# A hand-ordered attention and MLP kernel: state fetch and state transpose moved up in the head, and a new order of work for the first three batches

## The chip, the core and the metric

The kernel runs on one core of a Trainium2 chip. The core has four compute engines with queues of their own: TensorE (PE in the profile, with its weight loads shown apart as PEld), VectorE (DVE), ScalarE (ACT) and GpSimd (POOL). SyncE (SP) only issues DMA transfers; ACT and POOL issue some too. Each engine works through its own list of instructions in the order in which the kernel's source issues them, and waits at an instruction until the data and buffers that it needs are there.

The metric is the time of one execution on the device in microseconds. Before the change it is 201.53 us, the median of three runs between 201.45 and 201.57.

## The reference

Cut to what matters:

```python
B, H, S, Ns, D = 8, 8, 512, 32, 64            # batches, heads, tokens, state rows, head width
scores  = (x @ state^T) / sqrt(D)             # per batch and head: 512 x 32
a       = softmax(scores, -1);  xread = a @ state
scores2 = (state @ x^T) / sqrt(D)             # the same products, 32 x 512
a2      = softmax(scores2, -1); sread = a2 @ x
rows    = concat([xread, sread], tokens)      # 544 rows of 512 (heads x D) per batch
h       = rows @ w_in                         # 512 -> 2048
out     = maximum(0.01 * h, h) @ w_out        # 2048 -> 512
```

The inputs are x (8 MB, float32), the state, w_in and w_out (4 MB each, float32); the output has 4352 rows of 512 float32 numbers.

## The kernel before

The kernel never forms xread. For each batch it builds M = state times w_in (a 256 x 2048 matrix, in four column chunks c = 0 to 3; `a_m`, L381 to L398, an "M product" of eight small matmuls, whose PSUM tile is called `pm`), and the first layer is then `aT` (the transposed probabilities) times M: `ff1` (L409 to L421) makes one of 16 blocks j of 128 hidden units for 512 tokens in PSUM tile `ph`, and a leaky ReLU on ACT ("relu") moves it to `hT`. The second layer multiplies `hT` with `w_out`. For batch 0 it does this with plain matmuls, `piece(b, hT, i, jq)` (L693) for token tile i and hidden blocks 4*jq to 4*jq+3; `part` picks some of the four, and `y_store` moves a finished tile out. From batch 1 on it uses a scheme of seven products instead of eight (`Fast` and `Batch`), cut into 56 "units" of two matmuls each; `before.run(1)` or `u` issues one unit of the previous batch. That scheme needs sums of `w_out` blocks (`weights_sum(dst, m0, m1)`, L730, tiles `tw`, each half made on DVE or POOL) and sums of `hT` blocks (`before.f.sums`, DVE, tiles `su`).

Scores come from `a_scores(a)` (L219), which needs the transposed x (`xT`) and the transposed state. Batch 0 has its own path: `x0_t` transposes x on TensorE, scores and softmax are done in two halves of 256 tokens (`scores0` to `probs0`), and the first layer in quads of four blocks (`Quad`, L1036). For batch 1, `turn` (L1091) transposes x on TensorE. From batch 2 on, x is loaded (`load_x`, into `xl`), cast to bfloat16 head by head (`cast_x`, into `xb`; for batch 2 half on ACT, half on POOL) and transposed by DMA (`a_xt_dma`, L208). Softmax over state rows runs on DVE and ACT: `a_top`, `a_rows`, `a_less` (maximum and subtraction), `a_exp` (ACT), `a_probs` (sum, reciprocal, product: `aT`). Softmax over tokens: `a_max2` (DVE, `mcol`), `a_exp2` (ACT, one call per half), `a_probs2`; its result `e2` is transposed by DMA with `a_a2t`.

The states of batches 0 and 1 come in one transfer at the start. The states of batches 2 and 3 are group 0, those of 4 to 7 group 1: `load_state(i)` (L177) fetches a group in eight small transfers from SP into `stf`, and `state_t(i)` (L186) scales and casts it on POOL (`stb`) and issues a DMA transpose from SP into `st_t`. The memset of two columns of `stf[0]` on DVE (L1088) comes before the fetch of group 0, which overwrites them and therefore waits for it: the place of the memset in DVE's order is what starts the fetch.

Nothing plans this at run time. Order is written by hand: the head (batches 0 and 1, and the first half of batch 2) as a list of calls, and the stretches for b = 2 and later as strings of tokens, `FIRST` for b = 2 and `ORDER` after it. In these strings `u` is a unit, `f.j` an ff block, `r.j` its relu, `mk.c` an M product, `ev.c.g.A` or `.V` its cast by ACT or DVE, `S` the scores of the next batch, `tp`, `rw`, `ls`, `ex`, `x2`, `rc`, `ml` the parts of its softmax, `rows` the product of `e2` with x for finished batches (PSUM tile `psn`), `casts.h` two heads' casts on POOL, `st` is `state_t(1)`, `a2t` and `turn` are DMA transposes, `sb` and `sn` block sums, `d.n` the saving of product n (`d.1.A` by ACT), and `l4` the load of x for batch 4.

PSUM has eight banks: two for tag `ph`, two for `py`, and two each for the single tiles `big` and `sc`. A tile can be written again only when its last reader is done, which ties TensorE to ACT and DVE.

DMA transfers that POOL issues (`w_in`, `w_out`, x of batches 1 and 2) are all queued by 22 us, in this order at their end: `w_out` chunk 2, two halves of x of batch 2, two halves of `w_out` chunk 3.

Of the kernel before, what the change touches and what calls it, by code (L numbers as in the profile page):

```python
# [9 lines left out]
P = 128  # L10
# [20 lines left out]
def kernel(  # L31
# [100 lines left out]
    def load_w_out(c, parts=1):  # L132
        n = 4 // parts
        for j in range(4 * c, 4 * (c + 1), n):
            nc.gpsimd.dma_start(
                w_out_bf[:, j:j + n, :],
                moe_w_out[P * j:P * (j + n), :].rearrange("(j p) f -> p j f", p=P),
            )
# [147 lines left out]
    def a_top(a):  # L286
        a.m1 = block_max(a.sc[:].rearrange("p g c -> p (g c)"), NB)
# [582 lines left out]
    pxt = {}  # L870

    def x0_t(u, k):
        b = k // 3
        if (u, b) not in pxt:
            pxt[u, b] = psum.tile([P, 3 - 2 * b, 2, P], BF16, name="pxth", tag=("ph", "py")[u])
# [36 lines left out]
    def spread0(dst, parts, start):  # L912
        for i, part in enumerate(parts):
            for q in range(2):
                for v in range(2):
                    for c in range(NK):
                        n = H * v + NK * q + c
                        nc.tensor.matmul(
                            dst[NS * c:NS * (c + 1), q, P * v:P * (v + 1)],
                            lhsT=part[:, n:n + 1].to_broadcast([P, NS]),  # L920
                            rhs=ident[:], start=start, stop=start or (q == v == i == 1),
                        )
# [8 lines left out]

    def split0(m, eng):
        hi = att.tile([P, NG], BF16, name="hi0", tag="hi0")
        VEC(hi[:], m[:])
        lo = att.tile([P, NG], BF16, name="lo0", tag="lo0")
        with nc.allow_low_precision(reason="the second of two parts of one fp32 value"):
            eng.tensor_tensor(out=lo[:], in0=m[:], in1=hi[:], op=ALU.subtract)
        return hi, lo
# [19 lines left out]
    def recip0(u):  # L958
        q = att.tile([P, NG], BF16, name="q0", tag="q0")
        with nc.allow_low_precision(reason="one rounding, of the finished reciprocal"):  # L960
            nc.vector.reciprocal(q[:], r0[u][:])
        return q

    def recip0_rows(u, q):
        qb0[u] = psum.tile([P, 2, HT], FP32, name="qb0", tag="ph")
        spread0(qb0[u], (q,), True)
# [6 lines left out]
    for c in range(3):  # L973
        load_w_in(c)
    cast_x0(0, 0, NT, VEC)
    for k in (1, 2):
        cast_x0(k, 0, 2, VEC)
    for k in (1, 2):
        cast_x0(k, 2, NT, VEC)
    cast_x0(3, 0, 2, VEC)  # L980
    cast_x0(3, 2, NT, POO)
    for u, k in ((0, 0), (1, 0), (0, 1), (0, 2), (1, 1), (1, 2), (0, 3), (1, 3)):
        x0_t(u, k)
    for u in range(2):
        xt0_evict(u, 0, SCA)
        xt0_evict(u, 1, VEC)
# [3 lines left out]
    for v in range(2):  # L990
        scores0(0, v)
        max0(0, v)
    m = split0(m0[0], nc.gpsimd)
    load_w_in(3)
    load_w_out(0)
    for u in range(2):
        nc.gpsimd.dma_start(
            a1.xb[:, NK * u:NK * (u + 1)].rearrange("p h t d -> p h (t d)"),
            x[1, NK * u:NK * (u + 1)].rearrange("h (p t) d -> p h (t d)", t=NT),
        )  # L1000
    load_w_out(1, 2)
    load_w_out(2)
    for h in (0, NK):
        load_x(2, nc.gpsimd, h, h + NK)
    load_w_out(3, 2)
    rows0(0)
    scores0(1, 0)
    max0(1, 0)
    rows0(1)
    spread0(scn[0], m, False)  # L1010
    exp0(0)
    scores0(1, 1)
    max0(1, 1)
    for u in range(2):
        eps0(u)
    pm = a_m(a0, 0, "big")
    SCA(a0.M[:, 0, :DM], pm[:, 0, :])
    sum0(0)
    m = split0(m0[1], nc.vector)
    q = recip0(0)  # L1020
    spread0(scn[1], m, False)
    exp0(1)
    recip0_rows(0, q)
    VEC(a0.M[:, 1, :DM], pm[:, 1, :])
    probs0(0)
    pm1 = a_m(a1, 0, "sc")
    sum0(1)
    q = recip0(1)
    pm = a_m(a0, 1, "big")
    for g in range(2):  # L1030
        SCA(a0.M[:, g, DM:2 * DM], pm[:, g, :])
# [33 lines left out]
    def m0_evict(c, pm):  # L1065
        for d in range(DM * c, DM * (c + 1), 2 * P):
            VEC(a0.M[:, :, d:d + 2 * P], pm[:, :, d - DM * c:d - DM * c + 2 * P])

    first = Quad(0, 0, "py")
    first.product(range(2))  # L1070
    recip0_rows(1, q)
    probs0(1)
    m_evict(a1, 0, pm1, VEC)
    first.product(range(2, 4))
    first.relu()
    for u, j, tag in (
        (0, 4, "ph"), (1, 0, "big"), (1, 4, "py"), (0, 8, "ph"), (1, 8, "py"), (0, 12, "ph"), (1, 12, "big"),
    ):
        quad = Quad(u, j, tag)
        quad.product()  # L1080
        quad.relu()
# [32 lines left out]
    piece(0, h0, 1, 0)  # L1114
    piece(0, h0, 0, 0)
    a_exp2(a0, 0)
    turn(0)
    open_xb(2)
    weights_open()
    wide = psum.tile([P, 2, DM], FP32, name="pyw", tag="big", bufs=1)  # L1120
    VEC(a1.xT[:, :, 0:2, :], pt[0][:])
    turn(1)
    a_exp2(a0, 1)
    piece(0, h0, 2, 0, bank=wide[:, 0])
# [5 lines left out]
    m_take(a1, 1, 0, SCA)  # L1130
# [5 lines left out]
    piece(0, h0, 3, 1, copy=None, part=(0, 1))  # L1136
    piece(0, h0, 1, 1, copy=None, part=(0, 1))
    weights_sum(2, 0, 4, nc.gpsimd)
    a_open(a2, 2)
    m_take(a1, 1, 1, VEC)  # L1140
    m_take(a1, 2, 0, SCA)
    piece(0, h0, 3, 1, copy=None, part=(2, 3))
    piece(0, h0, 3, 2, copy=None, part=(0, 1))
    piece(0, h0, 2, 2, copy=None, part=(0, 1))
# [7 lines left out]
    cast_x(2, 4, 5, POO)  # L1152
    cast_x(2, 5, 6, POO)
    cast_x(2, 6, 7, POO)
    a_max2(a1)
    a_probs(a1, 0)
    a_probs(a1, 1)
    cast_x(2, 7, 8, POO)
    weights_sum(2, 4, 8)
    a_xt_dma(a2, slice(1, 2))  # L1160
    weights_sum(1, 4, 8)
    weights_sum(3, 4, 8, nc.gpsimd)
    a_exp2(a1, 0)
    weights_sum(1, 0, 4, nc.gpsimd)
    weights_sum(0, 4, 8, nc.gpsimd)
# [3 lines left out]
    piece(0, h0, 2, 2, copy=None, part=(2, 3))  # L1169
    piece(0, h0, 0, 1, copy=None, part=(2, 3))  # L1170
    cast_x(3, 0, 2, POO)
    a_exp2(a1, 1)
    piece(0, h0, 3, 2, copy=None, part=(2, 3))
# [404 lines left out]
```

## Time and profile before

| | before |
|---|---|
| median of three runs | 201.53 us (201.45 to 201.57) |
| the profiled execution's own time | 201.61 us |
| its span, first to last instruction | 199.8 us |
| TensorE busy | 193.8 us (97%) |
| DVE, ACT, POOL busy | 164.8, 150.1, 63.9 us |
| mean granted TensorE clock | 0.998 |
| moved by DMA | 27.50 MB |

In rows of the timeline the columns are: start in us from the span's start, duration in us, engine, line of the kernel (L181 is line 181), operation, output tile <- input tiles, shape, number of instructions merged into the row, and in brackets how long the engine had been idle before it and what ended that. A merged row's duration is the busy time of its instructions. The tile view gives the time "to landing" of a DMA transfer, counted from the start of its issue instruction; a transfer has landed when its consumers may read it. In the table by stretches, each engine's busy time in that stretch is followed by its number of instructions, and the DMA share is that of the core's 16 DMA engines.

### The profile page before, as it was taken

To read this page: it belongs to the slowest core of one execution; us is meant where nothing else is said; L and a number is where in the kernel's file an instruction comes from. 1 tells how busy PE (TensorE), PEld (TensorE's weight loads), DVE (VectorE), ACT (ScalarE), POOL (GpSimd) and SP (SyncE) were. 2 spreads that over 40 slices of the span, in tenths; PEclk is the share of its full clock that TensorE was granted. 3 is DMA by queue.
4 is the path that set the end of the run, shared out by engine and by line. 5 is a ranking of instruction groups with operands and counts; after the bars stand their busy time and mean duration, and the time that the engine had idled before them with its cause. 6 is when DMAs were issued, how large, how long until landed. Compare 5 with 4: busy or idle time off the path is not lost.

```text
span 199.8 us, 5151 instructions
## 1 busy us (share of the span) xinstructions
PE 193.8 (97%) x2106; PEld 136.5 (68%) x2106; DVE 164.8 (82%) x282; ACT 150.1 (75%) x286; POOL 63.9 (32%) x90
## 2 busy tenths in 40 slices
PE   7999998999999999999999999999999999999993
PEld 2566533446677667767777777777777788799882
DVE  2676498599999998997999899999899877995613
ACT  3478628599779649997899779996999768767710
POOL 8473284790009102720413040500050024005350
PEclk9999999999999999999999999999999999999999
DMA  6999997999571998398293614080013401310026
GB/s 203 212 207 192 199 292 136 206 318 162 101 220 27 197 276 165 58 255 268 51 259 113 184 22 85 3 262 0 3 51 159 82 3 76 134 56 0 5 82 182
DMA packets 40616, 27.50 MB, mean 138 GB/s; under 512 B 25424, under 2 KB 37840, under 8 KB 40592
## 3 DMA queue, kind: packets, MB, share of 16 engines
q1 hardware_dynamic: 34032, 20.35, 39.7%
q0 software_dynamic: 5728, 6.03, 16.8%
q10 hardware_dynamic: 832, 0.79, 1.2%
q8 instruction: 16, 0.26, 0.6%
q14 instruction: 8, 0.07, 0.1%
HBM read 17.30 MB, written 8.91 MB: 131 GB/s over the span
## 4 chain that ended last, share of the span: by engine, by line
PE 90%; DMA 4%; DVE 3%; POOL 0%; issue 0%; ACT 0%; ACTq 0%
PE yq L770 43%; PE ph L414 18%; PE pm L393 4%; PE pf L492 3%; PE yu L770 3%; PE pl L660 3%; PE ph L1051 3%; DMA st_t<-stb 2%; DMA xf<-in_x_dram 2%; PE py L699 2%; PE pl L581 2%; PE pyw L699 1%; PE psn L359 1%; PE sc L225 1%; PE php L1051 1%; PE phw L427 1%
## 5 line engine op out<-in xcount | busy, mean ns | idle before, releaser
L420 ACT ACTIVATE hT<-ph 128x512 bf16<-128x512 f32 x84 | 49.1, 608 | 14.3 <-PE ph L414 14.3
L770 PEld LDWEIGHTS <-su 128*128 128x128 bf16 x480 | 46.2, 98 | 12.4 <-ACT hT L420 0.4
L414 PE MATMUL ph<-aT,M 128*128 128x512 bf16 x168 | 47.9, 379 | 0.0
L770 PEld LDWEIGHTS <-hT 128*128 128x128 bf16 x336 | 32.3, 98 | 12.0 <-issue 2.7
L770 PE MATMUL yq<-tw_xf,su 128*128 128x256 bf16 x224 | 30.8, 273 | 0.0
L770 PE MATMUL yq<-w_out_bf,hT 128*128 128x256 bf16 x224 | 29.2, 273 | 0.0
L114 POOL CAST xb<-xl 128x512 bf16<-128x512 f32 (+1 forms) x24 | 15.2, 673 | 20.9 <-DMA xl<-in_x_dram 20.9
L414 PEld LDWEIGHTS <-M 128*128 128x128 bf16 x168 | 16.0, 98 | 7.7 <-issue 1.9
L759 DVE TENSOR_TENSOR su<-hT 128x1024 bf16<-128x1024 bf16 x28 | 19.1, 686 | 2.6 <-ACT hT L420 2.5
L842 POOL TENSOR_TENSOR yo<-sv,sv 128x512 f32<-128x512 f32 x7 | 9.3, 1330 | 37.2 <-ACT e L313 31.4
L1283 ACT CAST M<-pm 128x512 bf16<-128x512 f32 x30 | 16.8, 596 | 0.6 <-PE pm L393 0.6
L779 ACT COPY sv<-yq 128x512 f32<-128x512 f32 x24 | 14.0, 587 | 3.4 <-PE yq L770 3.3
L770 PE MATMUL yq<-tw_x,su 128*128 128x256 bf16 x112 | 16.3, 273 | 0.0
L770 PE MATMUL yq<-w_out_bf,su 128*128 128x256 bf16 x112 | 15.3, 273 | 0.0
L782 DVE TENSOR_TENSOR yo<-yq,sv 128x512 f32<-128x512 f32 x20 | 13.5, 677 | 2.1 <-PE yq L770 2.1
L770 PE MATMUL yq<-tw_x,hT 128*128 128x256 bf16 x104 | 13.9, 273 | 0.0
L313 ACT ACTIVATE e<-sc,mcol 128x512 bf16<-128x512 f32 x16 | 11.2, 704 | 0.2 <-DVE mcol L307 0.2
L699 PEld LDWEIGHTS <-hT 128*128 128x128 bf16 x64 | 5.9, 98 | 7.4 <-issue 0.9
L759 DVE TENSOR_TENSOR su<-su,hT 128x1024 bf16<-128x1024 bf16 x14 | 10.6, 755 | 0.2
L672 ACT COPY ls<-pl 128x512 f32<-128x512 f32 x16 | 9.5, 592 | 1.5 <-PE pl L660 1.0
L307 DVE TENSOR_REDUCE mcol<-sc 128x2 f32<-128x1024 f32 x8 | 9.7, 1216 | 0.0
L235 DVE TRANSPOSE_TENSOR_REDUCE mrow<-sc 128x32 f32<-128x1024 f32 x7 | 8.7, 1243 | 0.5 <-PE sc L225 0.5
(193 smaller groups left out, 350.8 us busy)
## 6 DMA issues: line engine op xcount, KB each, us to landing
xl<-in_x_dram SPq DMA_DIRECT2D x5, 1024.0 KB, 6.6
out_dram<-yo SPq DMA_DIRECT2D x10, 512.0 KB, 2.9
w_in_bf<-in_moe_w_in_dram POOLq DMA_DIRECT2D x4, 512.0 KB, 7.9
out_dram<-yo SPq DMA_DIRECT2D x7, 256.0 KB, 2.7
w_out_bf<-in_moe_w_out_dram POOLq DMA_DIRECT2D x2, 512.0 KB, 12.8
w_out_bf<-in_moe_w_out_dram POOLq DMA_DIRECT2D x4, 256.0 KB, 13.1
xl<-in_x_dram POOLq DMA_DIRECT2D x2, 512.0 KB, 15.4
out_dram<-ysb SPq DMA_DIRECT2D x4, 256.0 KB, 4.0
```

What stands on the lines that cost most here:

```text
L114: copy(xs[b][:, h0 // NK, :, h0 % NK:h0 % NK + h1 - h0].rearrange("p t h d -> p h t d"), xl[b][:, h0:h1].rearrange("p h (t d) -> p h t d", ...
L307: nc.vector.tensor_reduce(out=a.m2[:], in_=a.sc[:], axis=AX.X, op=ALU.max, negate=True)
L313: nc.scalar.activation(out=a.e2[:, g], in_=a.sc[:, g, :], func=AF.Exp, bias=a.m2[:, g:g + 1], accum_out=a.r2[:, g:g + 1],)
L414: nc.tensor.matmul(ph[:], lhsT=a.M[:, g, P * j:P * (j + 1)], rhs=a.aT[:, g, :], start=(g == 0), stop=(g == 1),)
L420: nc.scalar.activation(out=hT[:, j, :], in_=ph[:], func=AF.Prelu, scale=1.0 / SCALE, alpha=0.01)
L672: copy(self.sv[n], flat)
L699: nc.tensor.matmul(y.py, lhsT=hT[:, j, P * i:P * (i + 1)], rhs=w_out_bf[:, j, :], start=(j == 0), stop=(j == 15),)
L759: (eng or nc.vector).tensor_tensor(out=S[n][:, ms], in0=u[:, ms], in1=v[:, ms], op=op)
L770: nc.tensor.matmul(bank[:, i, :], lhsT=lhs[:, m, P * i:P * (i + 1)], rhs=rhs[:, m, :], start=(first and m == 0 and (i == 0 or of is not No ...
L779: copy(t[:], bank)
L782: nc.vector.tensor_tensor(out=dst, in0=bank, in1=self.sv[n][:], op=ALU.add)
L1283: copy(t.M[:, g, DM * c:DM * (c + 1)], src[g][:] if isinstance(src, list) else src[:, g, :])
```

## The change

The head is cut into finer steps and issued in another order, and `FIRST` is another order of the same tokens; `ORDER` and all that follows it are the same. No arithmetic changes. In particular:

- The memset of `stf[0]` and `load_state(0)` are issued after the casts of batch 0's M chunk 2 (`m0_take(2, ...)`) instead of after those of chunk 3 and, for the fetch, after the copies of batch 1's `xT`. `state_t(0)` follows at once, which puts it on POOL ahead of the two half sums `weights_sum(0, 0, 4)` and `weights_sum(2, 0, 4)`; these two change places.
- The first cast of batch 0's x is split in two. Pieces 0 and 1 of batch 0's output swap places; `a_exp2(a0, 0)` goes ahead of the last three relus of batch 0.
- For batch 1, the scores go ahead of the M product of chunk 1; both casts of chunk 1 are on ACT and both of chunk 2 on DVE, ahead of `a_max2`. The M product of batch 2's chunk 0, the first user of `st_t`, goes ahead of batch 1's chunk 3.
- POOL casts the first four heads of batch 3 before its last half sum `weights_sum(0, 4, 8)` instead of after it. On SP, the transpose of batch 0's `e2` and four of the eight fetches of group 1 are issued sooner.
- In `FIRST`, three units stand between `rows` and the pair `mk.3`, `S`; softmax steps, sums and casts are placed anew; two M casts go from ACT to DVE and two from DVE to ACT.

The diff, cut to the order (the new small functions `hi0`, `lo0`, `quad`, `m0_make`, `m0_half`, `m0_take` and `load_x1` wrap steps that the kernel before wrote out or looped over):

```diff
-    def m0_evict(c, pm):
-        for d in range(DM * c, DM * (c + 1), 2 * P):
-            VEC(a0.M[:, :, d:d + 2 * P], pm[:, :, d - DM * c:d - DM * c + 2 * P])
+    def m0_take(c, i):
+        d = DM * c + 2 * P * i
+        VEC(a0.M[:, :, d:d + 2 * P], pm0[c][:, :, 2 * P * i:2 * P * (i + 1)])
...
-        if (u, j) == (1, 0):
-            m0_evict(2, a_m(a0, 2, "sc"))
-        if (u, j) == (0, 8):
-            pm = a_m(a0, 3, "big")
-            a_scores(a0)
-            m0_evict(3, pm)
-            nc.vector.memset(stf[0][:, 0, D - 1:D + 1], 0.0)
-            a_max2(a0)
...
-    piece(0, h0, 1, 0)
-    piece(0, h0, 0, 0)
-    a_exp2(a0, 0)
-    turn(0)
...
-    VEC(a1.xT[:, :, 2:4, :], pt[1][:])
-    load_state(0)
-    m_make(a1, 1, "ph")
-    a_scores(a1)
...
-    weights_sum(0, 0, 4, nc.gpsimd)
-    m_make(a1, 2, "ph")
...
-    weights_sum(2, 0, 4, nc.gpsimd)
-    a_open(a2, 2)
-    m_take(a1, 1, 1, VEC)
-    m_take(a1, 2, 0, SCA)
...
-    a_top(a1)
-    state_t(0)
-    a_rows(a1)
-    a_less(a1)
-    a_exp(a1)
-    m_take(a1, 2, 1, SCA)
+    cast_x0(0, 0, 2, VEC)
+    cast_x0(0, 2, 4, VEC)
...
+    pm0[2] = a_m(a0, 2, "sc")
+    quad(2)
+    m0_take(2, 0)
+    m0_take(2, 1)
+    nc.vector.memset(stf[0][:, 0, D - 1:D + 1], 0.0)
+    load_state(0)
+    state_t(0)
+    qd[2].relu()
...
+    quad(5)
+    quad(6)
+    a_exp2(a0, 0)
+    qd[5].relu()
+    qd[6].relu()
+    piece(0, h0, 0, 0)
+    piece(0, h0, 1, 0)
+    turn(0)
...
+    a_exp2(a0, 1)
+    a_scores(a1)
+    m_make(a1, 1, "ph")
+    m_take(a1, 1, 0, SCA)
...
+    m_take(a1, 1, 1, SCA)
+    weights_sum(2, 0, 4, nc.gpsimd)
+    weights_sum(0, 0, 4, nc.gpsimd)
...
     a_exp(a1)
-    m_take(a1, 2, 1, SCA)
+    m_take(a1, 2, 0, VEC)
+    m_take(a1, 2, 1, VEC)
     cast_x(2, 0, 4, SCA)
...
     cast_x(3, 0, 2, POO)
+    piece(0, h0, 0, 2, copy=None, part=(2, 3))
+    cast_x(3, 2, 4, POO)
+    weights_sum(0, 4, 8, nc.gpsimd)
     a_exp2(a1, 1)
...
+    m_make(a2, 0, "sc")
     m_make(a1, 3, "ph")
-    cast_x(3, 2, 4, POO)
-    m_take(a1, 3, 0, SCA)
-    m_make(a2, 0, "sc")
-    m_take(a1, 3, 1, SCA)
+    piece(0, h0, 2, 3, copy=None, part=(0, 1))
+    piece(0, h0, 0, 3, copy=None, part=(0, 1))
     piece(0, h0, 3, 3, copy=None, part=(0, 1))
     ff(0)
...
     FIRST = (
-        "u l4 u f.1 f.0 sb.0.4 u sb.2.0 u f.2 r.1 r.0 d.1.A r.2 sb.1.4 d.2 sb.2.4 rows mk.3.big "
-        "casts.0 S u u f.3 u u u u u ev.3.0.A u u u u f.4 casts.2 r.3 tp d.6.A r.4 f.5 u sb.3.4 "
...
+        "f.1 l4 sb.2.0 u sb.0.4 a2t u f.0 u u f.2 rows r.1 r.0 d.1.A u u u mk.3.big S sb.1.4 f.4 "
+        "f.3 d.2 sb.2.4 r.2 casts.0 u u u u u u u f.7 ev.3.0.A r.4 r.3 tp sb.3.0 sb.3.4 rw d.6.A "
...
```

More of the change, by code (lines that the diff above doesn't have):

```diff
@@ L910, in rows0, with spread0 @@
                 )
[L912 to L922, printed above, removed]
+    def spread0(dst, part, start, last=True):
+        for q in range(2):
+            for v in range(2):
+                for c in range(NK):
+                    n = H * v + NK * q + c
+                    nc.tensor.matmul(
+                        dst[NS * c:NS * (c + 1), q, P * v:P * (v + 1)],
+                        lhsT=part[:, n:n + 1].to_broadcast([P, NS]),
+                        rhs=ident[:], start=start, stop=start or (last and q == v == 1),
+                    )
     def max0(u, v):
@@ L930, in max0 @@
         )
[L932 to L938, printed above, removed]
     def exp0(u):
@@ L971, in probs0 @@
         )
[L973 to L986, printed above, removed]
     a0.aT = att.tile([P, 2, S], BF16, name="aT", tag="aT")
```

320 lines of the change are left out of this document (189 added, 131 removed), and 10 rows, old and new, of the table FIRST.

## Prediction

> **What bounds the kernel now.** I read the page first, then the table by stretches, then TensorE's timeline and the chain. The page's head and its slices of TensorE:
>
> ```profile
> span 199.8 us, 5151 instructions
> PE 193.8 (97%) x2106; PEld 136.5 (68%) x2106; DVE 164.8 (82%) x282; ACT 150.1 (75%) x286; POOL 63.9 (32%) x90
> PE   7999998999999999999999999999999999999993
> ```
>
> TensorE is the bound: 97% busy and full in nearly every slice. Stretches (columns: TensorE, weight loads, DVE, ACT, POOL, clock, DMA share, GB/s):
>
> ```profile
> 30.00:32.00 2.00, 2.00 (x11) 0.92 (x10) 2.00 (x2) 2.00 (x3) 0.63 (x1) 1.00 1.19 220
> 33.00:34.00 1.00, 1.00 (x12) 0.27 (x10) 0.96 (x2) 0.57 (x2) 0.80 (x3) 1.00 0.21 36
> 34.00:35.00 1.00, 0.11 (x8) 0.00 (x0) 0.44 (x2) 0.82 (x2) 0.00 (x0) 1.00 0.05 9
> 36.00:60.00 24.00, 24.00 (x212) 13.89 (x210) 21.55 (x31) 19.81 (x38) 8.58 (x8) 1.00 0.88 201
> ```
>
> Between the head and the tail only 34 to 35 is empty. After 36 TensorE never stops, so there a new order can win almost nothing and can lose. The timeline shows the hole, and the chain its cause:
>
> ```profile
> 33.70 0.41 PE L393 MATMUL pm<-w_in_bf,st 64*32 64x512 bf16 x8
> 35.07 0.41 PE L393 MATMUL pm<-w_in_bf,st_t 64*32 64x512 bf16 x8 [0.96 <-DMA st_t<-stb]
> 39.40 0.41 PE L225 MATMUL sc<-xT,st_t 64*32 64x512 bf16 x8
> ...
> 30.66 4.37 DMA st_t<-stb
> 38.61 0.86 PE ph L414 x4
> ```
>
> The second product is batch 2's, the first user of st_t. One group of eight small matmuls follows another after 0.22 us (52.21 to 52.43, quoted below), so that product could have begun at 33.92: the stall is 1.15 us. A 128x512 matmul takes 0.86/4 = 0.215 us.
>
> **The change, part by part.** *States and their transpose.*
>
> ```profile
> 15.91 1.29 DVE L1067 CAST M<-pm 128x512 bf16<-128x512 f32 x2 [0.80 <-PE pm L393]
> 19.62 3.63 SPq L181 DMA_DIRECT2D stf<-in_state_dram  x8
> DMA to landing us min/median/max: 4.9/5.0/5.2
> 25.59 2.11 POOL L736 TENSOR_TENSOR tw_xf<-w_out_bf 128x1024 bf16<-128x1024 bf16 x1 [3.25 <-DMA w_out_bf<-in_moe_w_out_dram]
> 27.67 2.12 POOL L736 TENSOR_TENSOR tw_x<-w_out_bf 128x1024 bf16<-128x1024 bf16 x1
> 29.77 0.86 POOL L187 TENSOR_SCALAR stb<-stf 128x256 bf16<-128x256 f32 x1
> 32.37 1.43 POOL L114 CAST xb<-xl 128x256 bf16<-128x256 f32 x4 [1.74 <-DMA xl<-in_x_dram]
> ```
>
> The memset that gates the eight fetches goes behind the casts of 15.91, so SP issues them from 17.25 instead of 19.62; the last begins 3.2 later, at 20.45, and lands 5.2 after that, at 25.7 (third row: the fetches' time to landing). On Pool, stb now stands ahead of the two sums. It waits for the fetches while the sums, queued behind it, wait for w_out until 25.59 anyway; it ends at 26.6, and the transpose issues at 26.65. Its own 4.37 puts it at 31.0, before the 33.70 at which batch 2's product (now first of the two) wants it. The nearest rows give bounds of 4.4 and, from the fetches, 5.2; an issue to landing of 7.0 would still do. The sums end at 30.85 instead of 29.8; the next work on Pool waits for x of batch 2 until 32.37, so this 1.05 costs nothing. Without that cover the casts of x would slip by it.
>
> On SP, batch 0's e2 transpose and four fetches of later states move up, but stay behind the 1 MB load of batch 3; their users stand after 51. Cost 0.
>
> *What is late next: x of batch 2.* Without the stall the same matmuls reach the scores of batch 2 at 39.40 - 1.15 = 38.25. They read xT:
>
> ```profile
> L209 SPq DMA_TRANSPOSE xT<-xb x2: 1232/1262/1291, 33.8 to 35.2; - x2
> DMA to landing us min/median/max: 3.2/3.4/3.6
> ```
>
> The two xT transposes issue at 33.8 and 35.2; the second lands at 38.8. They follow Pool's casts (32.37 + 1.43), and these the load of x, which nothing here brings forward: the DMA share is 1.19 before it. Now the transpose of 64 KB of states runs ahead of that load. The xT transposes of 256 KB each land 1.8 apart (37.0, 38.8), so 64 KB are 0.45 at most; 0 at least, if they fit between the loads. I take 0.2, the middle, and the scores start at 39.0: a new wait of 0.75 in place of 1.15. All of TensorE's later work is queued behind it, and DVE's row maximum of batch 2 waits for it; small delays ahead of it disappear in it.
>
> *DVE, to the probabilities of batch 1.* a_scores(a1) goes ahead of an M product, but both casts of M chunk 2 are DVE's now, ahead of max2:
>
> ```profile
> 27.65 0.41 PE L393 MATMUL pm<-w_in_bf,st 64*32 64x512 bf16 x8
> 29.63 1.21 DVE L307 TENSOR_REDUCE mcol<-sc 128x2 f32<-128x1024 f32 x1
> 33.46 0.88 DVE L274 TENSOR_TENSOR aT<-e,qb 128x1024 bf16<-128x1024 bf16 x1
> 35.86 0.59 PE L414 MATMUL ph<-aT,M 128*128 128x512 bf16 x2
> ```
>
> Chunk 2's product stands six matmuls later (27.65 + 1.3 = 28.95). If its cast starts 0.5 after it, two casts at 1.29/2 each put max2 at 30.7, 1.07 later than now, and aT at 34.34 + 1.07 = 35.4. ff 0 is reached at 35.86 - 1.15 + 4 x 0.215 = 35.57, for four matmuls more stand before it. Cost 0; the cover is 0.15, and behind that the 0.75 at the scores.
>
> *Head.* One cast of x0 becomes two, 0.2 at most, before the same wait for a load. Output pieces 0 and 1 swap, equal parts. a_exp2(a0,0) goes ahead of three relus:
>
> ```profile
> 19.50 1.22 DVE L307 TENSOR_REDUCE mcol<-sc 128x2 f32<-128x1024 f32 x1
> 21.19 1.02 ACT L1060 ACTIVATE hT<-php 128x1024 bf16<-128x1024 f32 x1
> 23.82 0.55 PEld L699 LDWEIGHTS <-hT 128*128 128x128 bf16 x4
> ```
>
> It waits for mcol (20.72), takes 0.7; the relus, 1.0 and 1.0, end at 23.5 instead of 22.2, before TensorE wants their bank at 23.82. Cost 0; beyond that cover, up to the 0.3 that the later wait does not swallow.
>
> *The first stretch.* The rows of batch 0, the last M chunk and the scores of batch 3 stood together; now three units part the rows from the others.
>
> ```profile
> 51.33 0.59 PE L414 MATMUL ph<-aT,M 128*128 128x512 bf16 x2
> 51.86 0.42 PE L359 MATMUL psn<-xb,a2T 128*32 128x64 bf16 x32
> 52.21 0.41 PE L393 MATMUL pm<-w_in_bf,st_t 64*32 64x512 bf16 x8
> 52.43 0.40 PE L225 MATMUL sc<-xT,st_t 64*32 64x512 bf16 x8
> 52.76 0.61 PE L770 MATMUL yq<-tw_xf,su 128*128 128x256 bf16 x4
> 50.67 1.09 ACT L420 ACTIVATE hT<-ph 128x512 bf16<-128x512 f32 x2 [0.19 <-PE ph L414]
> ```
>
> Entering small tiles costs 51.86 - 51.33 - 0.43 = 0.10, leaving them 52.76 - 52.43 - 0.22 = 0.11: a second visit is +0.2. ACT had only 0.19 to spare there, and ff 2 and the sixth product's first unit now ask for its results about 0.2 sooner: 0 to +0.3, taken as 0, since its total is the same. Four M casts trade ACT (0.6) and DVE (0.68), two each way: 0. Every later stretch has the same order.
>
> Sum: -1.15 + 0.75 + 0.20 = -0.20 us. Against the profiled execution's 201.61 (span 199.8 and 1.8 around it) that is 201.41; the median of the runs, 201.53, stands 0.08 lower: 201.33, said as 201.3.
>
> **The rivals.** *A, the whole stall goes.* If x of batch 2 lands 0.75 sooner, no wait takes the stall's place: -0.95, 200.6. For it: the loads have gaps after 33 (share 0.21), so an end lags. Against: 1.19 before that leaves little room.
>
> *B, the transpose is no sooner.* st_t landed at 35.03, just after the last w_out load (21.6 + 13.2 = 34.8):
>
> ```profile
> 21.62 0.71 POOL L135 DMA_DIRECT2D w_out_bf<-in_moe_w_out_dram  x1 [0.96 <-DMA xb<-in_x_dram]
> DMA to landing us min/median/max: 13.2/13.2/13.2
> ```
>
> If it came last because queued loads stood before it, it lands there again. The product of 33.70 waits 1.35, the scores start at 39.6: +0.2 + 0.2, so 201.9. Against it: the fetches landed amid the loads. The Trainium skill, "DMA: Bandwidth & Descriptors", section "Queues, rings and completion order", has each DMA engine take the queue rows in turn, a packet at a time; by that the transpose passes the backlog, and the sum stands.
>
> *C, the transpose holds up x: the slower side.* At 34 to 35 the DMA share was 0.05, yet the last load was reported only then, 0.25 before st_t: a load that shares the engines with a transpose may be reported with it. Between 27 and 33 the load so held is x of batch 2, and Pool's casts, xT and the scores slip with it. Slower than before begins with x 0.2 later than my 32.57 (32.37 + 0.2), slower by 0.2% with 0.6. With st_t at 31.9 and an end that lags by 1.3, as the last load's did behind the busy stretch (33 to 34.3 and later), x comes at 33.2: scores at 39.65, +0.25 + 0.2, 202.0. The same section of the Trainium skill says that a semaphore's increment lands only after every earlier write of that DMA engine, across its queues. The late report agrees; no run here shows it for x.
>
> *D, Pool's third sum.* It now stands between the casts of batch 3.
>
> ```profile
> 40.62 2.14 POOL L736 TENSOR_TENSOR tw_xf<-w_out_bf 128x1024 bf16<-128x1024 bf16 x1
> 42.78 2.28 POOL L114 CAST xb<-xl 128x512 bf16<-128x512 f32 x4
> 45.87 1.87 SPq L209 DMA_TRANSPOSE xT<-xb  x1
> DMA to landing us min/median/max: 6.0/6.0/6.0
> ```
>
> The casts may start no sooner than 42.78, so with the sum inside they end at 47.2, and xT of batch 3 issues then. It lands at 52.2 if it takes the 5.0 of batch 2's pair, at 53.2 with its own 6.0. Its scores are wanted at 39.0 + (52.43 - 39.40) + 0.2 + three units of 0.22 = 52.9: a wait of 0 to 0.35, up to 201.7; beyond 0.2% only if the load of batch 3 slips too.
>
> **How the numbers follow.** Forecast 0.38 (its own range 201.1 to 201.7), A 0.15, B 0.16, C 0.21, D 0.10. This kernel's measurement tells 0.2%, 0.4 us, from no change. With x not delayed at all the forecast gives 201.1, so 0.11 of it is faster and 0.27 the same; A is faster; B stands at the bound, 0.08 each side; C is 0.18 slower, 0.03 the same; D 0.07 the same, 0.03 slower. Faster 0.26, same 0.45, slower 0.29. The range runs from A to C, with a part of ACT's 0.3 on top: 200.5 to 202.2.
>
> **What would show it.** Fetches from 17.3; stb before the sums; st_t landed by 32; no wait at batch 2's product; a wait of 0.5 to 0.9 for DMA xT before the scores near 39; a lone psn group. Wrong if x of batch 2 reaches Pool far from 32.5, if TensorE still waits for st_t, or if new waits show between 39 and 53.

## The result and the profile after

The changed kernel takes 202.06 us (median of 22 runs, 201.7 to 203.22) against 201.43 us of the kernel before in the same sitting. The ratio is 1.0028, with a 95% interval from 1.0017 to 1.0040: slower by 0.3 to 0.8 us. A second sitting gave 1.0026 (1.0010 to 1.0042). The forecast was 201.3 us. Its range holds the time; its direction is wrong.

The profiled execution of the changed kernel took 201.78 us (span 200.0). The page's head and its slices of TensorE:

```profile
span 200.0 us, 5151 instructions
PE 194.5 (97%) x2106; PEld 136.9 (68%) x2106; DVE 164.6 (82%) x284; ACT 149.7 (75%) x285; POOL 63.3 (32%) x90
PE   7999999999999999999999999999999999999993
```

The hole that showed as an 8 in the seventh slice is gone from this view, and the kernel is no faster for it. TensorE came to it later: in this profile it ran 0.73 us behind the kernel before from batch 0's scores on (18.75 against 18.02; the last section says why), so it waited 0.17 us for the states' transpose instead of 0.96. In another profile of the changed kernel, e16 below, the whole wait is back (timeline of TensorE):

```profile
35.21 0.41 PE L399 MATMUL pm<-w_in_bf,st_t 64*32 64x512 bf16 x8 [0.96 <-DMA st_t<-stb]
```

The timeline of the first profile of the changed kernel, all engines, over the same stretch (start, duration, engine, line, operation; in brackets the idle time before and what ended it):

```profile
17.98 4.66 SPq L187 DMA_DIRECT2D stf<-in_state_dram  x8
...
27.84 0.86 POOL L193 TENSOR_SCALAR stb<-stf 128x256 bf16<-128x256 f32 x1 [5.23 <-DMA stf<-in_state_dram]
28.68 2.11 POOL L742 TENSOR_TENSOR tw_x<-w_out_bf 128x1024 bf16<-128x1024 bf16 x1
28.72 1.26 SPq L194 DMA_TRANSPOSE st_t<-stb  x1
30.77 2.11 POOL L742 TENSOR_TENSOR tw_xf<-w_out_bf 128x1024 bf16<-128x1024 bf16 x1
...
32.84 1.42 POOL L114 CAST xb<-xl 128x256 bf16<-128x256 f32 x4
34.28 2.62 SPq L215 DMA_TRANSPOSE xT<-xb  x2
...
34.67 0.41 PE L399 MATMUL pm<-w_in_bf,st_t 64*32 64x512 bf16 x8 [0.17 <-DMA st_t<-stb]
...
39.21 0.41 PE L231 MATMUL sc<-xT,st_t 64*32 64x512 bf16 x8
```

And the chain of waits of the changed kernel in that stretch (start, duration, what):

```profile
22.21 5.16 DMA stf<-in_state_dram
...
27.84 0.87 POOL stb L193
28.71 0.02 issue
28.72 5.90 DMA st_t<-stb
34.62 0.04 issue
34.67 0.63 PE pm L399 x16
```

The order is as intended: Pool makes stb ahead of the two sums, and SP issues the transpose at 28.72, 1.94 us sooner than before. But the transpose now takes 5.90 us instead of 4.37 and lands at 34.62 instead of 35.03. Batch 2's first M product starts at 34.67 (35.07 before), and the scores of batch 2 at 39.21 (39.40 before). From product to scores it is 4.54 us now; it was 4.33.

Why the transpose is late shows in the DMA queues (packets, MB, share of the 16 engines). Q0 carries the loads that Pool issues, q1 what SP issues. First the changed kernel from 28.8 to 32 us, then the same kernel from 32 to 34.7:

```profile
q0 software_dynamic: 511, 0.80, 111.8%
q8 instruction: 1, 0.02, 2.1%
```

```profile
q0 software_dynamic: 152, 0.14, 30.9%
q1 hardware_dynamic: 288, 0.07, 12.5%
```

From its issue until 32 us the transpose moved not one packet, while 511 packets of Pool's loads ran. All its 288 packets ran from 32 us on, as the loads ran out; the last load landed at 34.39. In the kernel before, where the transpose was issued at 30.66, the window from 32 to 34.7 us holds the same 288 packets:

```profile
q1 hardware_dynamic: 288, 0.07, 11.8%
```

Issued sooner, it waited longer.

Two further differences lie behind the scores. The rows now stand apart in the stretch of batch 2 (timeline of TensorE, changed kernel):

```profile
51.58 0.42 PE L365 MATMUL psn<-xb,a2T 128*32 128x64 bf16 x32
...
52.04 0.81 PE L776 MATMUL yq<-tw_xf,su 128*128 128x256 bf16 x6
...
52.79 0.41 PE L399 MATMUL pm<-w_in_bf,st_t 64*32 64x512 bf16 x8
...
53.01 0.40 PE L231 MATMUL sc<-xT,st_t 64*32 64x512 bf16 x8
```

And in this execution TensorE lost 0.26 us in front of a quarter product of batch 3, which begins at 84.50 although the four units of 83.81 were through at 84.24:

```profile
83.81 0.60 PE L776 MATMUL yq<-w_out_bf,su 128*128 128x256 bf16 x4
...
84.50 0.38 PE L666 MATMUL pl<-lq,M 128*128 128x256 bf16 x2
```

From the scores of batch 2 to those of batch 4 it is 32.93 us (39.21 to 72.14), before 32.83 (39.40 to 72.23).

### The profile page after: what moved, and what is told of

The parts are those of the page before. It is cut to its first block, busy times and chain, and to the rows that moved or that the text cites. A ratio compares the mean times of both kernels' runs of the same rounds, so it can differ in the third digit from the quotient of the medians.

```text
span 200.0 us, 5151 instructions
## 1 busy us (share of the span) xinstructions
PE 194.5 (97%) x2106; PEld 136.9 (68%) x2106; DVE 164.6 (82%) x284; ACT 149.7 (75%) x285; POOL 63.3 (32%) x90
## 4 chain that ended last, share of the span: by engine, by line
PE 84%; DMA 6%; DVE 4%; SPq 2%; ACT 2%; issue 1%; POOL 0%; POOLq 0%
PE yq L776 41%; PE ph L420 17%; PE pm L399 4%; PE pf L498 3%; PE yu L776 3%; DMA st_t<-stb 3%; PE pl L666 3%; DMA stf<-in_state_dram 3%; PE pspin L149 2%; SPq L187 2%; PE pl L587 2%; DVE su L765 1%; PE psn L365 1%; PE ph L1002 1%; PE sc L231 1%; PE py L705 1%
## 5 line engine op out<-in xcount | busy, mean ns | idle before, releaser
L765 DVE TENSOR_TENSOR su<-hT 128x1024 bf16<-128x1024 bf16 x28 | 20.0, 719 | 2.8 <-ACT hT L426 2.8
L765 DVE TENSOR_TENSOR su<-su,hT 128x1024 bf16<-128x1024 bf16 x14 | 9.6, 687 | 0.2
L261 ACT ACTIVATE e<-sh 128x1024 bf16<-128x1024 f32 x7 | 7.4, 1061 | 2.7 <-DVE sh L254 2.5
```

The source lines that it names most:

```text
L765: (eng or nc.vector).tensor_tensor(out=S[n][:, ms], in0=u[:, ms], in1=v[:, ms], op=op)
```

## The experiments

Several theories are named in the expectations. Q: the transpose of the states lands with the last load that Pool has queued, and the end of the kernel hangs on that landing plus a fixed distance. P: the loss sits in the head, in the order of the two M products behind the transpose. D or F: it sits in later rows. X: what is late next, behind the states, is batch 2's transposed input xT. Ratios are to the kernel before in the same sitting.

**e1_pair.** The order of the two M products undone.

```diff
-    m_make(a2, 0, "sc")
     m_make(a1, 3, "ph")
+    m_make(a2, 0, "sc")
...
-    m_take(a2, 0, 0, SCA)
     m_take(a1, 3, 0, SCA)
+    m_take(a2, 0, 0, SCA)
```

> The changed kernel with the two M products in their old order: batch 1's last one ahead of batch 2's first, and their first evictions in that order. Theory Q (the transpose of the states lands with the last queued load of weights, so the end hangs on that landing plus a fixed distance): batch 1's product fills time in which TensorE waits anyway, the scores of batch 2 start 4.33 us after the landing as before the change instead of 4.54, and the kernel is 0.2 us faster than the changed one: about 201.85 us, ratio 1.0018. Theory D (the loss has nothing to do with that stall and sits only in later rows): no difference, 202.06 us.

Measured: 201.67 us, ratio 1.0006 (0.9989 to 1.0023). Timeline of TensorE:

```profile
34.43 0.41 PE L399 MATMUL pm<-w_in_bf,st 64*32 64x512 bf16 x8
35.16 0.41 PE L399 MATMUL pm<-w_in_bf,st_t 64*32 64x512 bf16 x8 [0.32 <-DMA st_t<-stb]
39.49 0.41 PE L231 MATMUL sc<-xT,st_t 64*32 64x512 bf16 x8
```

The transpose landed later here (28.43 issued, 35.12 landed), but from the product to the scores it is 4.33 us again. The interval overlaps that of the changed kernel (1.0017 to 1.0040), so the time alone does not show the effect; the distance does. Its 0.21 us are the pair's: batch 1's product, which needs no transpose, fills a wait when it stands first, and delays the work behind when it stands second.

**e2_rows.** The rows put back beside mk.3 and the scores of batch 3.

```diff
-        "... f.2 rows r.1 r.0 d.1.A u u u mk.3.big S ..."
+        "... f.2 r.1 r.0 d.1.A u u u rows mk.3.big S ..."
```

> The changed kernel with the rows of the states put back beside the scores of batch 3 (rows, mk.3, S together). Forecast's third term (parting them costs TensorE two more switches between tile shapes, 0.20 us): 0.2 us faster, about 201.86 us. Rival: the pitch of those matmuls is made up by idle time elsewhere and nothing changes, 202.06 us. In the trace the distance from the scores of batch 2 to the scores of batch 3 shows it: 0.2 us less, or the same.

Measured: 202.15 us, ratio 1.0039 (1.0024 to 1.0055), no gain. The distance from the scores of batch 2 to those of batch 4 grew to 33.28 us (39.27 to 72.55), for a wait appeared where the rows had stood (timeline of TensorE):

```profile
52.10 0.82 PE L776 MATMUL yq<-tw_xf,su 128*128 128x256 bf16 x6 [0.39 <-ACT sv L785]
```

At that place the rows cover a wait of the units. Putting this one piece back is no clean test of its price.

**e3_state_alone.** The kernel before, with the memset, the fetches and the transpose of the states at their new places, and nothing else.

> The kernel before with only the states of batches 2 and 3 fetched sooner and their transpose issued ahead of the block sums. The forecast's theory (the transpose lands 4.4 to 5.9 us after its issue): issue about 28.7 us or sooner, landing at 33.1 to 34.6 us instead of 35.03, TensorE's stall of 1.15 us shrinks by the same, 0.4 to 1.15 us faster: 200.3 to 201.0 us. Theory Q (it lands with the last queued load of weights, 34.4 to 34.8 us whatever its issue): landing between 34.4 and 35.0 us, 0 to 0.4 us faster, ratio 0.998 to 1.000.

Measured: 201.65 us, ratio 1.0011 (1.0001 to 1.0020). Timeline:

```profile
27.90 1.26 SPq L188 DMA_TRANSPOSE st_t<-stb  x1
...
34.93 0.41 PE L393 MATMUL pm<-w_in_bf,st_t 64*32 64x512 bf16 x8 [0.63 <-DMA st_t<-stb]
```

Issued 2.76 us sooner than before, the transpose took 7.0 us and landed at 34.89, behind a last load of 34.71. The one part of the change that was to bring the gain brings none. That is theory Q against the forecast.

**e4_no_last_loads.** The changed kernel without the last two queued loads; Pool fills that quarter with zeros.

```diff
-    load_w_out(3, 0)
-    load_w_out(3, 1)
+    nc.gpsimd.memset(w_out_bf[:, 12:16, :], 0.0)
```

> The changed kernel with the last two queued loads (the last quarter of the output weights, which land at 32.91 and 34.39 us) left out; GpSimd fills that quarter with zeros in its idle time, so the product of the second layer is made with zeros there. Theory Q: the transpose lands right behind the second half of batch 2's input, at about 32 us instead of 34.62, TensorE doesn't wait for it any more, the M product starts when TensorE is free (33.6 to 34.3 us), and the kernel is 0.3 to 1.0 us faster than the changed one: 201.0 to 201.75 us. The forecast's theory (the landing hangs on the issue): issue at 28.7 and landing at 34.6 us as now, 202.06 us.

Measured: 201.57 us, ratio 1.0011 (0.9998 to 1.0025). The queues from 28.8 to 32 us:

```profile
q0 software_dynamic: 114, 0.39, 36.4%
q1 hardware_dynamic: 288, 0.07, 10.0%
```

Now all 288 packets ran before 32 us, and the transpose landed at 32.32, behind the second half of batch 2's input (32.00), 3.9 us from its issue. E7, which leaves the same loads out, repeats it (issued at 28.38, landed at 32.39). The cause is the backlog. And the forecast's other half shows: TensorE no longer waits for the states, it waits for the input at the scores.

```profile
33.94 0.41 PE L399 MATMUL pm<-w_in_bf,st_t 64*32 64x512 bf16 x8
...
39.16 0.41 PE L231 MATMUL sc<-xT,st_t 64*32 64x512 bf16 x8 [0.60 <-DMA xT<-xb]
```

The scores start at 39.16 us, where they started with the stall.

**e5_first_back** and **e6_pair_and_first_back.** The changed kernel with the whole order of batch 2's stretch as before; in e6 the pair too.

> The changed kernel with the whole written-out order of the stretch of batch 2 (FIRST) put back as it was before; the head stays changed. Theory P (the loss sits in the head, in the order of the two M products behind the transpose): the distance from the scores of batch 2 to those of batch 4, 32.93 us after the change and 32.83 before, goes back to about 32.83, the distance from the transpose's landing to the scores of batch 2 stays at 4.54 us, and the time stays at 201.9 to 202.1 us. Theory F (the loss sits in that stretch): about 201.6 us.

> The changed kernel with both undone: batch 1's last M product ahead of batch 2's first again, and the written-out order of batch 2's stretch as it was before. What stays changed is the order in the head and the sooner fetch and transpose of the states. Theory P and theory F agree that nothing that costs is left: 201.4 to 201.65 us, as before the change and as the run with the states alone. If it stays at 202 us, the loss sits in the rest of the head.

Measured: e5 201.68 us, ratio 1.0014 (1.0004 to 1.0025); e6 201.52 us, 1.0007 (0.9995 to 1.0019). In e5 the distance from product to scores is 4.55 us (34.74 to 39.29), and from the scores of batch 2 to those of batch 4 it is 32.73 (39.29 to 72.02): 0.20 less than in the changed kernel, the price of that stretch's new order, and 0.10 less than before, which is a gain of the head behind the scores (no single row of it stands out). With both undone nothing measurable is left of the loss, so the rest of the head costs nothing that these intervals can tell. E6's own profile (202.09 us, one of its slower runs) shows a wait that the forecast had as a rival, batch 3's scores for their input:

```profile
52.83 0.41 PE L231 MATMUL sc<-xT,st_t 64*32 64x512 bf16 x8 [0.48 <-DMA xT<-xb]
```

**e7_no_last_loads_sums_late.** As e4, with the two sums behind the casts of batch 2's input, so that xT comes sooner.

> As the run without the last two loads (that quarter of the output weights is zeros), and GpSimd's two block sums follow its four casts of batch 2's input instead of preceding them. Without the last loads the scores of batch 2 waited 0.60 us for their input's transpose, issued at 34.00 and 35.33 us behind the casts. Theory X (the input's transpose is what is late next, and the sums set it): the casts start when the input has landed, at about 32.0 us instead of 32.6, the second transpose lands 0.6 us sooner, the wait goes, the scores start at about 38.6 us and the time is 0.4 to 0.6 us less than the 201.57 us of that run: about 201.0 us. Rival (the transpose's own 3.8 us grow instead, or the sums now stall VectorE's): scores at 39.16 us or later as there, 201.57 us or more.

Measured: 203.02 us, ratio 1.0079 (1.0058 to 1.0100). The casts did start sooner and xT landed at 38.13 instead of 39.12, but TensorE lost 2.07 us waiting for batch 1's probabilities. Timeline of VectorE, then of Pool:

```profile
33.54 2.14 DVE L270 TENSOR_SCALAR r<-r 128x32 f32<-128x32 f32 x1
...
36.85 1.42 DVE L280 TENSOR_TENSOR aT<-e,qb 128x1024 bf16<-128x1024 bf16 x1
```

```profile
33.52 2.13 POOL L742 TENSOR_TENSOR tw_x<-w_out_bf 128x1024 bf16<-128x1024 bf16 x1
35.61 2.12 POOL L742 TENSOR_TENSOR tw_xf<-w_out_bf 128x1024 bf16<-128x1024 bf16 x1
```

A VectorE operation on 128x32 elements took 2.14 us beside a sum of Pool of 2.13; in the changed kernel the same operation took 0.21. The product aT took 1.42 beside the second sum, and 0.69 in the changed kernel. So this run shows that the sums cannot stand there, and leaves open what a sooner xT alone is worth.

**e8_ff0_in_the_gap.** E3, with the first product of batch 1's first layer moved into the gap.

```diff
     m_make(a1, 3, "ph")
     cast_x(3, 2, 4, POO)
     m_take(a1, 3, 0, SCA)
+    ff(0)
     m_make(a2, 0, "sc")
     m_take(a1, 3, 1, SCA)
     piece(0, h0, 3, 3, copy=None, part=(0, 1))
-    ff(0)
```

> The kernel before with the states fetched sooner, and in addition the first product of batch 1's first layer (four matmuls of 512 columns, 0.85 us) ahead of batch 2's first M product instead of behind a piece of the second layer. It needs only batch 1's probabilities, which are written by 34.4 us, and neither the states' transpose nor the last weights. Theory Q: TensorE's gap from 33.9 to 34.9 us is filled by about 0.5 us from 34.4 on, batch 2's M product starts at about 35.25 us instead of 34.93, and the scores of batch 2 start 0.5 us sooner, at 38.75 us: 201.65 us of the run with the states alone goes to about 201.15 us. Rival: the scores then wait for their input's transpose (38.3 to 38.8 us) or for M's eviction and little or nothing is gained, 201.4 to 201.7 us.

Measured: 201.93 us, ratio 1.0022 (1.0011 to 1.0033): the rival. The waits of TensorE:

```profile
PE ph L414 <- ACT M L1109: 0.7, 1, 0.7
```

The two PSUM tiles for that product are held by batch 1's last M chunk until ScalarE has copied it out, so ff 0 started at 34.94, not 34.4; the M product followed at 35.46 and the scores at 39.54. My count of that product (four matmuls, 0.85 us) was wrong too: it is two, 0.43 us.

**e9_pair_alone** and **e10_rows_alone.** The kernel before with one edit each: the pair's order; the rows behind f.2, with one unit between them and mk.3. The diff of e10:

```diff
-        "... u f.2 r.1 r.0 d.1.A r.2 sb.1.4 d.2 sb.2.4 rows mk.3.big casts.0 S u u f.3 ..."
+        "... u f.2 rows r.1 r.0 d.1.A u r.2 sb.1.4 d.2 sb.2.4 mk.3.big casts.0 S u f.3 ..."
```

> The kernel before with one thing changed: batch 2's first M product stands ahead of batch 1's last one. Theory Q: TensorE stands from about 33.7 us until the states' transpose lands at 34.7 to 35.1 us with neither product made, so both follow it, the scores of batch 2 start 4.55 us behind the landing instead of 4.33, and the kernel is 0.2 us slower than before: ratio 1.001. If the pair costs more than its own 0.22 us: ratio 1.002, as putting it back in the changed kernel made it look (1.0028 to 1.0006). If the order is without effect: 1.000.

> The kernel before with one thing changed: in the stretch of batch 2 the rows of the states stand right behind the second product of that stretch, and one unit of the second layer stands between them and mk.3 and the scores of batch 3 (which they stood beside). The forecast's third term: two more switches between small and full tiles, 0.2 us: the distance from the scores of batch 2 to those of batch 4 grows from 32.83 to 33.03 us, ratio 1.001. Rival (the units there wait for VectorE's sums anyway, and the rows fill that wait): 32.83 us, ratio 1.000.

Measured: e9 201.83 us, ratio 1.0024 (1.0015 to 1.0033); e10 201.64 us, 1.0026 (1.0012 to 1.0041). Timeline of TensorE in e9:

```profile
34.85 0.41 PE L393 MATMUL pm<-w_in_bf,st_t 64*32 64x512 bf16 x8 [0.64 <-DMA st_t<-stb]
35.07 0.40 PE L393 MATMUL pm<-w_in_bf,st 64*32 64x512 bf16 x8
35.41 0.39 PE L699 MATMUL pyw<-w_out_bf,hT 128*128 128x512 bf16 x1
36.17 0.59 PE L414 MATMUL ph<-aT,M 128*128 128x512 bf16 x2 [0.38 <-DVE tw_xf L736]
```

Product to scores is 4.87 us (34.85 to 39.72), 0.54 more than before. 0.22 are the pair; the rest is the wait at ff 0. The row names VectorE, but ScalarE's copy of the last M chunk began only at 35.54 and freed the first tile 0.6 us later, at 36.14. In the changed kernel three half pieces stand ahead of ff 0 and hide that. In e10 the distance to the scores of batch 4 is 33.07 us (39.11 to 72.18), 0.24 more than before: the rows' term, near the 0.20 of the forecast. That is 0.0012 of the time, the low end of e10's interval; what else the ratio of 1.0026 holds, if anything, its profile does not show.

**e11_states_on_tensor_engine** and **e12_work_ahead_of_scores.** E3 with the states transposed by TensorE instead of a DMA; in e12 a half piece and ff 4 ahead of batch 2's scores as well.

```diff
+    def state_pe():
+        ps = psum.tile([P, 2, P], BF16, name="pstt", tag="ph")
+        for u in range(2):
+            nc.tensor.transpose(ps[:, u], stb[0][:, u], ident[:])
+        SCA(st_t[0][:], ps[:])
```

> The kernel before with the states of batches 2 and 3 fetched sooner, and their transpose made by TensorE (two 128 by 128 transposes into one PSUM tile and one copy by ScalarE, at 32 to 33.4 us) instead of a DMA behind the queued loads. Theory Q: the copy is there by 33.4 us whatever the loads do, TensorE's wait of 0.6 to 1.15 us in front of batch 2's M product goes, the two transposes cost it about 0.2 us, and the scores of batch 2 could start at about 38.6 us. Theory X on what is late next: they then wait for their input's transpose, which has landed at 38.3 to 39.1 us, so the start comes to 38.7 to 39.15 us instead of 39.3 to 39.4: 0.2 to 0.6 us faster than before, ratio 0.997 to 0.999. If the wait turns up again in front of the same product, theory Q is wrong.

> The kernel with the states' transpose on TensorE, and in addition a half piece of the second layer (0.43 us) and one product of the first layer (ff 4, 0.43 us) ahead of batch 2's scores instead of behind them, with the relu that frees the PSUM tile of ff 4. In the run without that move TensorE waited 0.64 us at the scores for their input, with that work lined up behind. Theory X (what is late next is the input's transpose, and TensorE can do other work until then): the wait goes, the scores start at about 39.4 us, the end comes 0.4 to 0.6 us sooner than there: ratio to before 0.998. Rival (what follows the scores on VectorE, 0.2 us later, or the relu, holds up later work by as much): ratio 1.000 to 1.001.

Measured: e11 201.63 us, ratio 1.0012 (0.9997 to 1.0027); e12 201.95 us, 1.0032 (1.0018 to 1.0046). Timeline of e11, then the waits of TensorE in e12:

```profile
32.87 0.37 ACT L195 COPY st_t<-pstt 128x256 bf16<-128x256 bf16 x1
...
34.12 0.40 PE L400 MATMUL pm<-w_in_bf,st_t 64*32 64x512 bf16 x8
...
39.25 0.41 PE L232 MATMUL sc<-xT,st_t 64*32 64x512 bf16 x8 [0.64 <-DMA xT<-xb]
```

```profile
PE yq L777 <- DVE ysb L716: 0.8, 1, 0.8
```

In e11 the states are ready in time and the M product waits for nothing, yet the scores start at 39.25: they wait for xT, which landed at 39.21. In e12 that wait is gone too, and TensorE waits for VectorE's copy of an output at 45.48 instead (0.78 us). The wait moved twice and the time never came below that of the kernel before.

**e13_changed_again** to **e17_before_third.** More profiles of the two kernels.

> The changed kernel once more, for a second profile and an interval beside the others'. By theory Q and the terms found so far (0.22 us for the pair, 0.20 for the rows, 0.10 gained at the output's copies) it is 0.32 us slower than before, ratio 1.0016, with the transpose of the states landing at 34.6 to 35.1 us, the scores of batch 2 at 4.54 us behind that, and 32.93 us from there to those of batch 4; if the loss is as large as first measured (1.0028), the profile has a further wait of 0.2 to 0.3 us, for instance for the first quarter product of batch 3 near 84 us, as in the first profile.

> The changed kernel, a third profile. If the rest of the loss is the wait near 84 us, it shows here in this and the fourth profile at least once more, with about 0.28 us, and the profiled time is near 202.0 us. If the rest is the landing of the states' transpose, that comes at 34.9 us or later, and the distances behind it are 4.54, 32.93 and 20.5 us.

> The kernel before, a second profile: the transpose of the states lands at 34.6 to 35.1 us as in all kernels that have it behind the queued loads, and the distances behind it are 4.35, 32.83 and 20.5 us, so that the profiled time is 201.2 to 201.6 us.

> The changed kernel, a fourth profile: as for the third, a wait near 84 us of about 0.28 us again, or a landing at 34.9 us or later, or neither.

> The kernel before, a third profile: as for the second, a landing at 34.6 to 35.1 us and distances of 4.35, 32.83 and 20.5 us behind it.

Times and places in us (ratio of e13 1.0026; the others are single runs). The landings are the issue plus the time to landing in the traces:

| profile | time | transpose issued | last load landed | transpose landed | product | product to scores | scores of batch 2 to 4 |
|---|---|---|---|---|---|---|---|
| before | 201.61 | 30.66 | 34.77 | 35.03 | 35.07 | 4.33 | 32.83 |
| before, e15 | 201.75 | 30.73 | 34.65 | 34.90 | 34.94 | 4.33 | 32.82 |
| before, e17 | 201.34 | 31.46 | 34.23 | 34.62 | 34.74 | 4.43 | 32.80 |
| changed | 201.78 | 28.72 | 34.39 | 34.62 | 34.67 | 4.54 | 32.93 |
| changed, e13 | 201.69 | 28.48 | 34.58 | 34.74 | 34.78 | 4.55 | 33.01 |
| changed, e16 | 202.07 | 28.57 | 35.01 | 35.17 | 35.21 | 4.55 | 32.94 |
| states alone, e3 | 201.65 (median) | 27.90 | 34.71 | 34.89 | 34.93 | 4.33 | 32.81 |

E14 took 204.32 us: its loads landed about 1 us later (the last at 35.41), xT at 41.61, and the scores of batch 2 waited 1.32 us for it. TensorE had lost 1.4 us in the head to a late load of w_in. The transpose again landed just behind the last load (35.68). It is the slowest of all runs of the two kernels (202.89 is the slowest of the kernel before); whether the change has a part in that, one run can't tell, and it is left out of the table. E15, a profile of the kernel before, has the wait near 84 us as well:

```profile
83.78 0.60 PE L770 MATMUL yq<-w_out_bf,su 128*128 128x256 bf16 x4
84.47 0.38 PE L660 MATMUL pl<-lq,M 128*128 128x256 bf16 x2
```

So that wait is not the change's: of the three profiles of each kernel in the table, one has it (e15 and the first profile of the changed kernel).

## Why the prediction was wrong

*The bound and the hole.* Right: TensorE bounds both kernels, and the hole was the wait for st_t. But its length belongs to the execution: in front of the product TensorE stood idle for 0.96 and 0.65 us in two profiles of the kernel before and not at all in the third (e17, where it came late), and for 0.17, 0.29 and 0.96 us in the three of the changed kernel. The 1.15 us of the forecast were those of one execution.

*The fetches and stb.* Partly right. The order on Pool came as said, but the fetches began at 17.98 instead of 17.25 (TensorE was late by 0.73 us in this profile; in e5, where it was not, they began at 17.32), the eight took 4.2 us to issue instead of 3.2, and the last landed at 27.38 instead of 25.7. So the transpose was issued 2.1 us later than forecast (28.72, not 26.65). That cost nothing: in e3 it was issued at 27.90 and landed at 34.89.

*The transpose: the step that failed.* "Its own 4.37 puts it at 31.0", within bounds of 4.4 and 5.2. Measured were 5.9 us in the changed kernel, 7.0 in e3 and 3.9 in e4, where the last loads are left out. The duration is no property of the transpose: it lands 0.16 to 0.39 us behind the last queued load in every row of the table, whether issued at 27.90 or at 31.46 (in e5 0.16 us ahead of it, at 34.70). The forecast's 4.37 already held about 2 us of waiting: the same transpose for the later states, issued at 63.1 us in the kernel before, took 2.41. So the -1.15 us of the sum, with the +0.75 that was to follow it, came to nothing. Rival B had this, and its price of 201.9 us is near what came (202.06, and 201.91 in the second sitting), but I gave it 0.16. I read the fetches that landed amid the loads as evidence against it. In the changed kernel SP's packets for the fetches did run beside Pool's (51 beside 631 from 20 to 22 us, though none from 18 to 20); the transpose's packets from 28.8 to 32 us did not. That the scores of batch 2 started at 39.21 in the first profile, near the 39.0 of the forecast, is luck: they did not wait for xT as forecast, but stood 4.54 us behind a product that waited for the states.

*Turns between the queues.* The Trainium skill, "DMA: Bandwidth & Descriptors", section "Queues, rings and completion order", has each DMA engine take the queue rows in turn, packet by packet. By that the transpose would have passed the backlog. In the changed kernel's trace it did not: no packet of q1 in 3.2 us beside 511 of q0. Later, and with a shorter backlog, packets of both queues did run in one window (288 beside 152 from 32 us on; 288 beside 114 in e4). What decides when the transpose gets its turn is not settled by any run here.

*x of batch 2.* The delay of 0.2 us did not show (31.83 landed, 32.31 before). The cover that I named for Pool's sums did go: they ended at 32.88 instead of 30.85, and the casts behind them slipped to 32.84, against 32.37 before. "Without that cover the casts of x would slip by it" is what happened, and 0.31 us of slack at the scores hid it.

*The new wait of 0.75 us for xT.* Right in mechanism, but out of reach while st_t stayed late: where the states were ready it appeared with 0.60 us (e4) and 0.64 us (e11). Part of that wait is a slower transfer: the second xT transpose took 3.79 us from issue to landing in e4 (35.33 to 39.12) and 4.14 in e11 (35.07 to 39.21), against 3.29 in the changed kernel (35.61 to 38.90). Why it took longer there is open. The forecast's net gain of 0.40 us from this pair of waits is not there either: those two kernels are at 1.0011 and 1.0012.

*The pair of M products.* Not a term of my sum; only rival B carried it, as +0.2. From product to scores it was 4.54 to 4.55 us in e5 and three profiles of the changed kernel, and 4.33 in e1 and two profiles before (4.43 in e17): 0.21 to 0.22 us, because the states came last.

*The parted rows, +0.20.* Right in size: 0.20 between e5, which undoes the whole stretch, and the changed kernel; 0.24 in e10, which moves little else. As e2 shows, it does not come back by moving the rows alone.

*The head's other edits, 0.* Right within what e6 can tell; 0.10 us were gained by one profile (e5). *Rivals C and D:* C did not occur. D's wait did not occur in the changed kernel, and showed as 0.48 us in e6.

The sum by the profiles: 0.22 + 0.20 - 0.10 = 0.32 us slower from the same landing. The first sitting gave 0.34 to 0.81 us (0.17% to 0.40% of 201.43), the second 0.20 to 0.85. The profiles account for the lower part of that. What else, if anything, separates the two medians stays open: the landing differs from run to run by 0.41 us before and by 0.55 us after, and three profiles of each are too few to show a difference of 0.2 us between them.

## What to carry to other kernels

A transfer's time from issue to landing is no price that moves with its issue: look in which window its packets run, and what else is in the queues then. If a wait ends together with the last of a backlog, issuing sooner only lengthens it; a shorter backlog (e4) or another engine for the work (e11) ends it. And before a hole is priced, follow the two or three arrivals behind it: in e4 and e11 the wait for the states went and one of 0.60 to 0.64 us for the input came, in e12 that went and one of 0.78 us for an output's copy came, and the end did not move forward. Work that needs nothing late belongs ahead of the wait, as batch 1's product does (4.33 us against 4.54), if nothing else holds it up: in e8 the tiles did.

## What the runs showed of the hardware

A sum on Pool held VectorE up. In e7 (rows above) VectorE's 128x32 operation, 0.21 us in the changed kernel, lasted until Pool's sum of two SBUF operands had ended, 2.14 us. The Trainium skill, "SBUF — State Buffer", section "Who interferes with whom", says that VectorE in its modes with two ports contends with GpSimd: whoever issues first holds the shared pair of ports for the whole instruction, and the other is fully blocked. E7 fits, with both ending within 0.03 us of each other (35.65 and 35.68); that VectorE's operation ran in such a mode, no run shows.

The first matmuls run at a slower pace for a time that differs from run to run, and the granted clock in the profile's table by stretches does not tell of it: it is 1.00 from 4 to 7 us in both. Three warm-up matmuls of 512 columns took 0.82 us in the profile before and 1.46 in the first one after, with the same work ahead of them; the timelines of TensorE, before and after:

```profile
4.61 0.82 PE L143 MATMUL pspin<-idle 128*128 128x512 bf16 x3
```

```profile
4.74 1.46 PE L149 MATMUL pspin<-idle 128*128 128x512 bf16 x3
```

The change is not needed for it: in e15, the kernel before, the three took 1.32 us, and in e5 and e16, with the changed head, 0.82. In the first profile after, TensorE reached the scores of batch 0 at 18.75 us, before at 18.02; in e5, with the quick start, at 18.09. The wait for st_t swallowed the 0.7 us. (E16 came to them at 18.52 for another reason: a wait of 0.70 us for a cast of x, 0.17 before.) A hole that absorbs such differences also absorbs small gains ahead of it.
